# Moving two loads of x to earlier bundles in a hand-scheduled convolution and channel-mix kernel

## The chip, the cores and the metric

The kernel runs on one core of one Trainium2 chip. The metric is device time in microseconds (us); of several runs the median is given. A core has five engines that run side by side, each its own list of instructions in order: TensorE (PE) for matmuls, VectorE (DVE), ScalarE (ACT), GpSimd (POOL), and SyncE (SP), which here only issues transfers. Transfers run on 16 DMA engines that all issuers share.

## The reference

The input x has 8 batches of 4160 tokens with 192 channels. First a causal convolution over 7 tokens, with one softmax-normalized filter for each of 8 heads of 24 channels; then an RWKV channel mix on its result y.

```python
w = softmax(weight)                              # 8 heads x 7 taps
y = causal_conv(x, w)                            # per head, along the tokens
y_prev = y shifted by one token
xk = mu_k * y + (1 - mu_k) * y_prev
xr = mu_r * y + (1 - mu_r) * y_prev
k = relu(xk @ w_k)                               # 192 -> 1024
v = (k * k) @ w_v                                # 1024 -> 192
out = sigmoid(xr @ w_r) * v                      # float32, (8, 4160, 192)
```

## The kernel before

The batches are worked in four pairs. For each pair the tokens go in steps of 512 (`steps`), and a step of two batches is cut into 8 slots, each a matmul of xk with one part of w_k. Four slots make a *bundle*; there are 65 bundles, numbered from 0, and the second half of the second pair's work begins with bundle 24, the third pair's work with bundle 32. The order of the work is written out by hand: tables (`early`, `mix_a`, `late` and others) hold, for each bundle, the functions to call, and `bundle_rest` emits one bundle, in the middle of the kernel always in the same way: on PE two slots of `k_mm` (L593), the first half of an output tile (`v_rows`, L681, tile ps_v), a slot, the gate's matmuls (`r`, L650), a slot, a convolution unit if one is due (`conv_sparse`, L364, tile ps_c), then the second half of `v_rows`. ACT empties the tiles (`k_relu` L605, `r_out` L661, the casts of L337). DVE squares (L619), multiplies the output (`v_out`, L697), and builds xk and xr from y (`diff` L536, `scale` L567, `add_y` L573).

The convolution runs ahead of this. Its input is cut into *groups* of tokens, numbered 0 to 12. Groups 6, 7 and 8 belong to the second pair, 9 and 10 to the third, and from 8 on each group holds 2080 tokens of both batches of the pair. A group goes through five stations, each at a bundle of its own:

- `x_tile` takes a tile for x (tag `xb`, two buffers, so group 9 takes the one that groups 6 and 7 used), writes two elements of it with a DVE memset (L125) and, where the group starts its batch, clears 32 rows on POOL (L127).
- `load_x` issues the loads from POOL, one call for each of the two batches of the pair: for a group at the start of its batch a small first piece (L148) and four large ones (L154) of up to 240 KB as written to the tile. Before the second batch's call, `tie_x` writes two elements of the second batch's part with a DVE memset (L113); the first large load of that batch has to wait for it, so that the loads cannot be issued before DVE has reached that place in its order.
- `conv_sparse` is called four times, for two heads each, at bundles 14 to 17 for group 8 and 22 to 25 for group 9. Each call reads both batches.
- `y_write` writes y to DRAM from SP, 8 transfers, at the end of the last of those bundles (17 for group 8, 25 for group 9).
- `y_read` reads it back with a transposing transfer, also from SP, in two halves: for group 8 at the end of bundles 19 and 22. `diff` reads the result two bundles before the step that needs it; for the first half of group 8 that is in bundle 22.

What stands in the table `early` is called first in its bundle. The DMA transfers of POOL carry eight completion counters in turn, and a transfer waits until the previous one on its counter is complete.

Of the kernel before, what the change touches and what calls it, by code (L numbers as in the profile page):

```python
# [14 lines left out]
def kernel(  # L15
# [719 lines left out]
    def at(table, b, fn, *a):  # L735
        table.setdefault(b, []).append((fn, a))
# [7 lines left out]
    for g, (p, base, nb, fb, on_pe) in enumerate(groups):  # L744
        if g < 3:
            continue
        if p == 0:
            xs = {3: [1, 1], 4: [2, 2, 3, 3], 5: [4, 4, 5, 5]}[g]
        elif g not in sparse:
            xs = [fb - 9] * 2 + [fb - 7] * 2  # L750
        else:
            xs = {8: [14, 15, 16, 17], 9: [22, 23, 24, 25]}.get(g, [fb - 13, fb - 11, fb - 9, fb - 7])
        for i, b in enumerate(xs):
            xt.setdefault(b, []).append((g, i))
        if not on_pe:
            at(late, xs[-1], y_write, g)
        if g in sparse:
            at(late, max(fb - 5, xs[-1] + 2), y_read, g, slice(0, 1), 2)
            at(late, fb - 2, y_read, g, slice(1, 2), 2)
            b, b1 = {8: (9, 12), 9: (18, 21), 10: (24, 25)}.get(g, (fb - 19, fb - 16))  # L760
            at(early, b, x_tile, g)
            at(early, b, load_x, g, (0,))
            b = b1
            at(early, b, tie_x, g, 1)
            at(early, b, load_x, g, (1,))
            continue
        if not on_pe:
            at(mix_c if g == 4 else late, xs[-1] + (1 if g < 6 else 2), y_read, g)
        if g > 4:

            b = {5: 1, 6: 3, 7: 7}.get(g)
            b = first_bundle[first_step[p]] + (-15, -11, -7, -3)[(g - 6) % 4] if b is None else b
            table = {5: mix_a, 7: mix_c}.get(g, early)
            at(table, b, x_tile, g)
            at(table, b, load_x, g)
    for s, (p, t0, L, n0, ns) in enumerate(steps):
        fb = first_bundle[s]
# [27 lines left out]
    for s, j, vb in quads:  # L805
        b = vb - (s == LAST)
        if 0 < s < LAST - 1:
            b = min(b, first_bundle[s + 2] - 2 + j)
# [255 lines left out]
```

## Time and profile before

| | |
|---|---|
| median of 3 runs | 420.95 us (418.74 to 421.1) |
| the profiled execution's own time | 419.52 us |
| its span, first to last instruction | 417.7 us |
| mean granted TensorE clock | 0.992 |
| busy share of PE, DVE, ACT, POOL | 97%, 89%, 85%, 14% |
| PE L681 (ps_v) | 4032 matmuls, 190.0 us |
| PE L593 (ps_k) | 1632 matmuls, 192.5 us |
| PE L364 (ps_c) | 640 matmuls, 10.0 us, 4.2 us idle before them |
| x loads from POOL, 240 KB each | 52, median 8.2 us from issue to landing |

The profile was taken from one execution; all its times are microseconds from the span's start. "Busy" is time in which an engine executes instructions, and matmuls overlap in the pipeline, so that their single times may sum to more than the time that passes. "Idle before" is time in which the engine stood still ahead of an instruction, and the releaser behind the arrow is what ended it. The granted clock is the share of its full clock that TensorE had.

### The profile page before, as it was taken

The page shows a single profiled execution, that of the slowest core. Times are in us where ns is not written, and L with a number is a line of the kernel's source. Part 1 is how long each engine was busy: PE and PEld are TensorE (multiplying, and loading weights), DVE is VectorE, ACT ScalarE, POOL GpSimd, SP SyncE. Part 2 cuts the span into 40 slices and gives each one's busy share as a digit, 9 for nine tenths or more (in the row PEclk, how much of TensorE's full clock was granted, in tenths as well). Part 3 has the DMA queues.
Part 4 walks back from the last instruction along what each step waited for, and adds up shares of the span by engine and source line. Part 5 has one row for each costly group of instructions (what it writes and reads, how often), then busy time and mean ns, then how long its engine had stood idle before and what let it go on. Part 6 is the DMA issues. An engine that isn't in the chain of part 4 may idle for free.

```text
span 417.7 us, 17418 instructions
## 1 busy us (share of the span) xinstructions
PE 404.1 (97%) x7669; PEld 304.2 (73%) x7670; DVE 372.2 (89%) x672; ACT 354.8 (85%) x426; POOL 57.4 (14%) x91
## 2 busy tenths in 40 slices
PE   7899999999999969999999999999999999999996
PEld 5567767777867746777777777777777787777895
DVE  5999799998999966899999999999999999999973
ACT  6899988889998857989898988988989788787781
POOL 8622022030021202203120020300000001000000
PEclk9999999999999988999999999999999999999999
DMA  9999989997729993998997999959432767212223
GB/s 146 193 196 186 194 193 202 233 195 177 158 58 191 232 230 70 190 233 185 194 147 164 196 188 201 168 139 213 119 111 66 204 158 156 78 52 66 77 78 115
DMA packets 139091, 66.35 MB, mean 159 GB/s; under 512 B 89332, under 2 KB 139016, under 8 KB 139016
## 3 DMA queue, kind: packets, MB, share of 16 engines
q1 hardware_dynamic: 95672, 48.32, 47.7%
q0 software_dynamic: 42544, 16.36, 33.8%
q8 instruction: 60, 0.98, 1.0%
q10 hardware_dynamic: 800, 0.57, 0.5%
q14 instruction: 15, 0.12, 0.1%
HBM read 33.29 MB, written 36.99 MB: 168 GB/s over the span
## 4 chain that ended last, share of the span: by engine, by line
PE 62%; DMA 3%; DVE 0%; issue 0%
PE ps_v L681 28%; PE ps_k L593 26%; PE ps_r L650 5%; DMA xb<-in_x_dram 3%; PE ps_c L364 1%; PE ps_v L633 1%; DVE o_sb L717 0%
## 5 line engine op out<-in xcount | busy, mean ns | idle before, releaser
L605 ACT ACTIVATE k_sb<-ps_k 128x1024 bf16<-128x1024 f32 x260 | 253.4, 1039 | 37.5 <-PE ps_k L593 36.8
L619 DVE TENSOR_TENSOR k<-k_sb 128x1024 bf16<-128x1024 bf16 x260 | 173.6, 688 | 25.6 <-ACT k_sb L605 25.5
L593 PE MATMUL ps_k<-xk,wk 64*128 64x512 bf16 (+1 forms) x1632 | 192.5, 368 | 1.6 <-DVE xk L573 1.5
L681 PE MATMUL ps_v<-wv,k 64*128 64x192 bf16 x4032 | 190.0, 244 | 0.2 <-DVE k L619 0.2
L681 PEld LDWEIGHTS <-k 64*128 64x128 bf16 x4032 | 169.6, 94 | 13.4 <-issue 5.0
L593 PEld LDWEIGHTS <-wk 64*128 64x128 bf16 x1632 | 83.9, 94 | 57.5 <-issue 4.2
L697 DVE TENSOR_TENSOR o_sb<-ps_v,r_sb 128x768 f32<-128x768 f32 x64 | 60.9, 951 | 8.9 <-PE ps_v L681 6.5
L154 POOL DMA_DIRECT2D xb<-in_x_dram x62 | 43.9, 718 | 143.6 <-DVE xb L113 59.8
L661 ACT ACTIVATE r_sb<-ps_r 128x768 bf16<-128x768 f32 x65 | 53.5, 825 | 8.8 <-PE ps_v L681 7.2
L337 ACT CAST y<-ps_c 128x960 bf16<-128x960 f32 (+2 forms) x84 | 52.8, 709 | 3.8 <-PE ps_c L364 3.8
L650 PEld LDWEIGHTS <-xr 64*128 64x128 bf16 x780 | 34.9, 94 | 14.9 <-issue 1.3
L650 PE MATMUL ps_r<-wr,xr 64*128 64x192 bf16 x780 | 43.3, 243 | 0.5 <-DVE o_sb L697 0.5
L567 DVE TENSOR_SCALAR xr<-d,mu 128x512 bf16<-128x512 bf16 (+1 forms) x102 | 36.0, 357 | 0.0
L536 DVE TENSOR_TENSOR d<-yT 128x1536 bf16<-128x1536 bf16 (+4 forms) x36 | 31.2, 867 | 2.1 <-ACT yT L423 1.5
L567 DVE TENSOR_SCALAR xk<-d,mu 128x512 bf16<-128x512 bf16 (+1 forms) x99 | 32.7, 360 | 0.1
L573 DVE TENSOR_TENSOR xr<-xr,yT 128x1536 bf16<-128x1536 bf16 (+1 forms) x33 | 31.1, 942 | 1.1
L573 DVE TENSOR_TENSOR xk<-xk,yT 128x1536 bf16<-128x1536 bf16 (+3 forms) x33 | 30.6, 927 | 0.1
L520 POOL COPY y_tail<-yT 128x195 bf16<-128x195 bf16 x4 | 2.9, 721 | 88.6 <-DMA yT<-y_dram 88.6
L364 PE MATMUL ps_c<-xb,toe 32*32 32x240 bf16 x640 | 10.0, 270 | 4.2 <-DMA xb<-in_x_dram 3.8
L364 PEld LDWEIGHTS <-toe 32*32 32x32 bf16 x640 | 4.4, 88 | 13.0 <-issue 11.9
L127 POOL MEMSET xb<- 32x384 bf16 x3 | 1.2, 408 | 63.5 <-DVE xb L125 56.2
L413 PEld LDWEIGHTS <-xb 128*32 128x32 bf16 (+3 forms) x264 | 4.9, 112 | 2.5 <-ACT xb L247 1.3
(58 smaller groups left out, 65.1 us busy)
## 6 DMA issues: line engine op xcount, KB each, us to landing
out_dram<-o_sb SPq DMA_DIRECT2D x128, 192.0 KB
xb<-in_x_dram POOLq DMA_DIRECT2D x52, 240.0 KB, 8.2
y_dram<-y SPq DMA_DIRECT2D x40, 195.0 KB
y_dram<-y SPq DMA_DIRECT2D x16, 210.0 KB
xb<-in_x_dram POOLq DMA_DIRECT2D x4, 228.0 KB, 5.6
xb<-in_x_dram POOLq DMA_DIRECT2D x4, 192.0 KB, 6.1
wk<-in_moe_w_k_dram POOLq DMA_DIRECT2D x4, 192.0 KB, 6.0
xb<-in_x_dram POOLq DMA_DIRECT2D x2, 216.0 KB, 5.1
```

What stands on the lines that cost most here:

```text
L154: nc.gpsimd.dma_start(out=xb[q0 : q0 + rows, lo:hi, s, :], in_=bass.AP(tensor=x.tensor, offset=x.offset + (b * S + t0 + lo * step) * D, ap ...
L337: nc.scalar.copy(out=bass.AP(tensor=y.tensor, offset=y.offset + d, ap=[y.ap[0], [m * 2 * D, 2], [2 * D, m], [Q, 2], [1, b - a]],), in_=bas ...
L536: nc.vector.tensor_tensor(out=shaped(s, diffs[s][:, cs, :L]), in0=y_of(s, cs, 1), in1=y_of(s, cs, 0), op=ALU.subtract)
L567: nc.vector.tensor_scalar(out=t[:, c, :L], in0=diffs[s][:, c, :L], scalar1=mu[:, i, c : c + 1], scalar2=None, op0=ALU.mult)
L573: nc.vector.tensor_tensor(out=o, in0=o, in1=y_of(s, sl, 0), op=ALU.add)
L593: nc.tensor.matmul(out=ps[:, i, f * L : (f + 1) * L], lhsT=wk[r, c, fs], rhs=xk[r, c, :L], start=c == 0 and f == 0, stop=c == NC - 1 and f ...
L605: nc.scalar.activation(out=k_sb, in_=ps.rearrange("p a b -> p (a b)"), func=AF.Relu)
L619: nc.vector.tensor_tensor(out=o, in0=i, in1=i, op=ALU.mult)
L650: nc.tensor.matmul(out=ps[:, i, k * D : (k + 1) * D], lhsT=xr[q, c, ts], rhs=wr[q, c, :], start=c == 0, stop=c == NC - 1,)
L661: nc.scalar.activation(out=r_sbs[s, j], in_=r_ps.pop((s, j))[:, :, 0 : 2 * D], func=AF.Sigmoid)
L681: nc.tensor.matmul(out=v_ps[s, j][:, bank, k * D : (k + 1) * D], lhsT=k2s[s][q, f, t * P : (t + 1) * P], rhs=wv[q, f, :], start=half == 0 ...
L697: nc.vector.tensor_tensor(out=o_sb.rearrange("p (b t) d -> p b (t d)", b=2), in0=v_ps.pop((s, j)), in1=r_sbs.pop((s, j)), op=ALU.mult,)
```

## The change

For group 9 the pair of bundles at which the loads of its two batches are called becomes (17, 18) instead of (18, 21). `x_tile` and the first batch's `load_x` move from bundle 18 to 17; `tie_x` and the second batch's `load_x` move from bundle 21 to 18. All stay first in their bundles. No other group's entry is touched.

```diff
         if g in sparse:
             at(late, max(fb - 5, xs[-1] + 2), y_read, g, slice(0, 1), 2)
             at(late, fb - 2, y_read, g, slice(1, 2), 2)
-            b, b1 = {8: (9, 12), 9: (18, 21), 10: (24, 25)}.get(g, (fb - 19, fb - 16))
+            b, b1 = {8: (9, 12), 9: (17, 18), 10: (24, 25)}.get(g, (fb - 19, fb - 16))
             at(early, b, x_tile, g)
             at(early, b, load_x, g, (0,))
             b = b1
             at(early, b, tie_x, g, 1)
             at(early, b, load_x, g, (1,))
             continue
```

## The prediction

> **What bounds the kernel now.** I read first the page's busy line and its forty slices. PE is busy for 97% of the span, so time can only come out of a place where PE waits or runs slowly; the other engines have 11% or more to spare.
>
> ```profile
> PE 404.1 (97%) x7669; PEld 304.2 (73%) x7670; DVE 372.2 (89%) x672; ACT 354.8 (85%) x426; POOL 57.4 (14%) x91
> PE   7899999999999969999999999999999999999996
> PEclk9999999999999988999999999999999999999999
> ```
>
> Between the two ends there is one dent: the fifteenth slice (146.2 to 156.6 us) holds a PE digit of 6, and in it and the next the granted clock falls to 8. Who is waited for there, the list of waits says (engine, line, releaser: total us, times, longest). Cut to 160 us and later, the same list has no PE wait at all.
>
> ```profile
> PE ps_c L364 <- DMA xb<-in_x_dram: 3.8, 2, 2.6
> ACT y L337 <- PE ps_c L364: 3.8, 1, 3.8
> ```
>
> Then PE's order of time. A bundle runs from one first-half ps_v burst to the next, so bundle 22 runs from 148.48 to 161.24; its convolution (L364) is the first unit of group 9, the third pair's first group.
>
> ```profile
> 148.48 1.50 PE L681 MATMUL ps_v<-wv,k 64*128 64x192 bf16 x32
> ...
> 150.55 0.29 PE L364 MATMUL ps_c<-xb,toe 32*32 32x240 bf16 x8
> 152.06 0.28 PE L364 MATMUL ps_c<-xb,toe 32*32 32x240 bf16 x4 [1.21 <-DMA xb<-in_x_dram]
> 154.95 0.59 PE L364 MATMUL ps_c<-xb,toe 32*32 32x240 bf16 x20 [2.61 <-DMA xb<-in_x_dram]
> 155.47 2.74 PE L681 MATMUL ps_v<-wv,k 64*128 64x192 bf16 x32
> ...
> 161.24 1.48 PE L681 MATMUL ps_v<-wv,k 64*128 64x192 bf16 x32
> 163.30 0.42 PE L364 MATMUL ps_c<-xb,toe 32*32 32x240 bf16 x32
> 163.66 1.49 PE L681 MATMUL ps_v<-wv,k 64*128 64x192 bf16 x32
> ```
>
> The same work in bundle 23 has no gap in its convolution. Which load was late, GpSimd's order of time says: the last four x loads before the stall are issued at 140.52, released by the memset of L113, which ties them to DVE's place in bundle 21.
>
> ```profile
> 122.73 0.41 POOL L127 MEMSET xb<- 32x384 bf16 x1 [34.61 <-DVE xb L125]
> 123.43 0.54 POOL L148 DMA_DIRECT2D xb<-in_x_dram  x1 [0.29 <-POOL xb L127]
> 123.96 2.75 POOL L154 DMA_DIRECT2D xb<-in_x_dram  x4
> 126.70 0.53 POOL L148 DMA_DIRECT2D xb<-in_x_dram  x1
> 140.52 2.75 POOL L154 DMA_DIRECT2D xb<-in_x_dram  x4 [13.29 <-DVE xb L113]
> ```
>
> They land up to 154.9 (the chain that ended last has this load as a piece of 12.32 us from 142.58). On SP the first transposing read of group 8 is issued at 136.93 for 5.93 us; from 142 to 144 the DMA view shows 2266 packets of SP's queue and none of GpSimd's, so the x loads stand behind it. The second such read is issued at 148.91.
>
> **The price of the stall.** By stages (us, then the five engines, PEclk, DMA share, GB/s):
>
> ```profile
> 148.48:161.24 12.76, 8.94 (x137) 6.00 (x134) 6.39 (x11) 6.53 (x8) 0.00 (x0) 0.73 0.98 192
> 161.24:167.47 6.23, 6.23 (x138) 4.46 (x134) 5.43 (x11) 5.90 (x10) 2.69 (x4) 1.00 0.33 40
> 167.47:173.89 6.42, 6.42 (x137) 4.57 (x134) 5.80 (x12) 6.42 (x10) 2.71 (x4) 1.00 1.33 182
> ```
>
> These bundles do the same PE work (137 or 138 matmuls in the records). Bundle 22 takes 12.76 - 6.23 = 6.53 us more than 23. By parts: the two waits are 1.21 + 2.61 = 3.82; from the second ps_v burst to the bundle's end it takes 161.24 - 155.47 = 5.77 against 167.47 - 163.66 = 3.81, so 1.96 for the slow clock; the convolution's own matmuls at that clock take the other 0.74. Bounds from neighbours: against bundle 24 the excess is 6.34; against bundle 16 (113.24 to 119.17, 5.93) it is 6.83.
>
> The clock part stands on a row: in the stage from 155.00 to 159.30 the granted clock is 0.50, after two idle pieces of 1.21 and 2.61 us. The Trainium skill ("TensorE: Matmul & The Clock Gate", section "HAM oscillation — how this bites in real kernels") asks for no idle gap above some 3.4 us; read strictly, gaps of 1.21 and 2.61 would leave the clock alone and only 3.82 us would come back. The trace disagrees, since the clock did fall, and I go by the trace.
>
> **The change part by part.** Nothing is added or removed; the order of the built kernels is the same on POOL, SP and ACT, and on DVE two memsets of 59 ns move.
>
> *First batch, 18 to 17.* The memset of L125 moves from 122.53 to its place between the last two squarings of the bundle before, about 116.1 (DVE starts a squaring at 115.41 and the next at 116.48, after 0.39 idle). The memset on POOL (0.41), one issue of L148 (0.54), four of L154 (2.75) and the second batch's first piece (0.53) follow, so issues run from about 116.9 to 120.7 instead of 123.43 to 127.2. POOL has idled since 88, so nothing is queued behind them. The buffer was last read by group 7's convolution, whose last matmul is at 95.7: no new wait on DVE or POOL. From 115 to 119 no DMA packet moves, so these 0.97 MB find empty engines; before, they went out beside group 8's write-back (SP, 123.24 for 8.77 us).
>
> *Second batch, 21 to 18.* The memset of L113 takes the old place of L125, 122.53, so the four L154 issue from 122.6 to 125.4, some 18 us earlier. The last of them waits on the counter of the first batch's first large load; with that issued near 117.4 and the landings of this batch before at 9.4 to 11.7 us, it would be held to at most 129.1. The slowest x load of the trace landed after 14.1 us: 143.2 at worst, against a need at 150.55. The wait is therefore gone, with 7 us to spare; the conv of bundles 23 to 25 reads the same tile and needs nothing more.
>
> *What the loads now stand beside.* Group 8's write-back at 123.24 has the second batch beside it in place of the first: the same four or five transfers, 0.96 against 0.97 MB. What can be added is what remains of the first batch by then: nothing, or at most all of it, 0.97 MB at the 200 GB/s of the stage 124 to 139, 4.9 us. I take 1 us, since it has six us of free engines. The write-back feeds the first transposing read, whose packets end near 144, and DVE wants it at 150.31 (L536): slack 6.2 us, so either bound is covered. Were that cover gone, each us late would stop DVE and then PE for one us. From 140 to 155 the output writes and both transposing reads lose a megabyte of competition; this is off PE's path and I count it as nothing.
>
> *What is late next.* Group 10's loads hang on DVE in bundles 24 and 25 and move 6.5 us forward with everything else, to about 158; the second transposing read, issued at 148.91, was through at 157.4 in spite of the x loads. Its reader is four bundles later. All later stages keep their mutual distances.
>
> **The sum.** Against the profiled execution (span 417.7, its own time 419.52): 3.82 + 1.96 + 0.74 = 6.52 less, hence 413.0 and a span near 411.2. Its time is 1.43 under the median of the runs shown (420.95); from the median it is 414.4. I take the middle, 413.7. The likeliest case alone spans 411.9 (fastest run 418.74 less 6.83) to 414.6 (median less 6.34).
>
> **The rivals.**
> 1. *The gain is only part.* The transposing read of group 8 slips past 150.31 and DVE waits at L536 in bundle 22. Against it: 6.2 us of slack against at most 4.9 of extra bytes; for it: the write-back's issues on SP took 0.33 to 2.1 us each, so SP's queue does stretch. At 8 to 10 us of slip, 2 to 4 us are lost and 413.7 becomes 416 to 418.
> 2. *Nothing to be had.* The unprofiled runs do not have this stall, because their loads land in time: 420 to 421. For it: landings hang on what else is in flight. Against: the profiled run is inside the range of the others, not above it.
> 3. *Slower.* The same place as in 1, but so crowded that the read is more than 6.2 + 6.5 = 12.7 us late: then a DVE stall and a cold PE cost more than the old wait. At 16 us it is 413.7 + 9.8, near 423.5, plus a clock loss like the 2.7 now: 426. It would need some three times the bytes that the change moves.
> 4. *The load moves but lands late again.* It would have to take 25 us from issue, against 14.1 at most; no chance worth naming.
>
> **How the numbers follow.** Likeliest case 0.78, rival 1 0.08, rival 2 0.08, rival 3 0.06. The range goes from 411.5, a little under the case's 411.9 since three runs do not bound the spread, up to 417.1, the median less the 3.82 of the waits alone (all clock loss back elsewhere), which takes in half of rival 1. One per cent, about what a measurement of this kernel tells from no change, is 4.2 us. Faster by more: 0.78 + 0.05 of rival 1 = 0.83; within: 0.03 + 0.08 + 0.02 of rival 3 = 0.13; slower: 0.04.
>
> **What would show it.** In the profile of the changed kernel: first x loads issued near 117 and the tied four near 122.6; no PE wait on x in the list; PE digits of 9 throughout the middle; granted clock 1.00 from 150 to 160; bundle 22 in 5.9 to 6.4 us; span near 411.2. I am wrong if DVE waits for the transposing read at L536, if the x wait turns up again at L364, or if the dent goes and the timed runs still stand near 420.

## The result, and the profile after

The changed kernel takes 414.66 us as the median of 4 runs (412.98 to 414.86), the kernel before, in 4 runs beside it, 420.65: a ratio of 0.9857, 95% interval 0.9817 to 0.9898. So it is 1.4% faster. In this document a median takes in every run of a kernel, while a ratio leaves out the few runs that lie more than 1.5% above the fastest of their kernel. Its profiled execution took 412.98 us with a span of 411.3, against 419.52 and 417.7 before.

The page's busy line and slices of the changed kernel:

```profile
PE 401.3 (98%) x7670; PEld 302.5 (74%) x7670; DVE 371.1 (90%) x672; ACT 354.6 (86%) x426; POOL 57.8 (14%) x91
PE   7899999999999999999999999999999999999996
PEclk9999999999999999999999999999999999999999
```

The 6 in the fifteenth slice is gone, and so are the two 8s of the clock. The same stretch in PE's order of time, and the stages of bundles 22 and 23 (us, busy time of PE, PEld, DVE, ACT, POOL, then PEclk, DMA share, GB/s):

```profile
148.52 1.50 PE L681 MATMUL ps_v<-wv,k 64*128 64x192 bf16 x32
150.59 0.42 PE L364 MATMUL ps_c<-xb,toe 32*32 32x240 bf16 x32
150.95 1.50 PE L681 MATMUL ps_v<-wv,k 64*128 64x192 bf16 x32
...
154.72 1.48 PE L681 MATMUL ps_v<-wv,k 64*128 64x192 bf16 x32
```

```profile
148.52:154.72 6.20, 6.20 (x138) 4.53 (x134) 5.97 (x11) 5.99 (x8) 0.00 (x0) 1.00 0.72 173
154.72:161.05 6.33, 6.33 (x136) 4.59 (x134) 5.87 (x11) 6.33 (x10) 2.60 (x4) 1.00 0.54 111
```

Bundle 22 starts at 148.52, as before (148.48), runs its convolution in one piece of 0.42 us, and is over after 6.20 us instead of 12.76: 6.56 less, which is the whole gain of the span (6.4). From the end of bundle 25 to the end of the span it takes 411.3 - 173.70 = 237.6 us now, and took 417.7 - 180.13 = 237.6 before. The loads and the read, in the order of time of POOL and of SP:

```profile
116.41 0.41 POOL L127 MEMSET xb<- 32x384 bf16 x1 [28.12 <-DVE xb L125]
117.11 0.60 POOL L148 DMA_DIRECT2D xb<-in_x_dram  x1 [0.29 <-POOL xb L127]
117.70 2.77 POOL L154 DMA_DIRECT2D xb<-in_x_dram  x4
120.46 0.53 POOL L148 DMA_DIRECT2D xb<-in_x_dram  x1
123.09 2.89 POOL L154 DMA_DIRECT2D xb<-in_x_dram  x4 [2.10 <-DVE xb L113]
```

```profile
123.42 7.05 SPq L466 DMA_DIRECT2D y_dram<-y  x8
130.56 4.83 SPq L705 DMA_DIRECT2D out_dram<-o_sb  x4
135.48 7.52 SPq L488 DMA_TRANSPOSE yT<-y_dram  x1
```

The second batch's four large loads are issued 17.4 us earlier, and by the trace's packets the last x packet moves at 139.8 instead of 154.5. The first transposing read of group 8 (called *the read* from here on) has its last packet at 145.8, 1.4 us later than before (144.4), and DVE wants it at 150.35.

### The profile page after: what moved, and what is told of

Read it like the earlier page. It is cut to its first block, busy times and chain, and to the rows that moved or that the text cites. A ratio compares the mean times of both kernels' runs of the same rounds, so it can differ in the third digit from the quotient of the medians.

```text
span 411.3 us, 17419 instructions
## 1 busy us (share of the span) xinstructions
PE 401.3 (98%) x7670; PEld 302.5 (74%) x7670; DVE 371.1 (90%) x672; ACT 354.6 (86%) x426; POOL 57.8 (14%) x91
## 4 chain that ended last, share of the span: by engine, by line
PE 87%; DMA 4%; DVE 4%; ACT 2%; POOL 1%; issue 1%; SPq 0%; POOLq 0%; ACTq 0%
PE ps_v L681 39%; PE ps_k L593 37%; PE ps_r L650 7%; PE ps_c L364 2%; DMA yT<-y_dram 2%; DMA wk<-in_moe_w_k_dram 2%; DVE k L619 2%; PE ps_v L633 1%; ACT k_sb L605 1%; DMA y_dram<-y 1%; PE ps_c L319 1%; ACT y L337 0%; DVE d L536 0%; POOL xb L154 0%; SPq L479 0%
```

## The experiments

The table sums up what the profiles show of this one meeting place. "Loads" is when the second batch's large loads start to be issued, "read on SP" how long the read occupies SP's list; packets are those of the trace (256 bytes for the read, 384 for x), their times to within 0.1 us. The waits are those of bundles 20 to 22, in the one profiled execution of each kernel.

| kernel, bundles of group 9 | loads | read on SP | read's packets | last x packet | waits, us |
|---|---|---|---|---|---|
| before (18, 21) | 140.52 | 5.93 | 139.0-144.4 | 154.5 | PE for x 3.8 |
| after (17, 18) | 123.09 | 7.52 | 137.5-145.8 | 139.8 | none |
| first only (17, 21) | 141.14 | 3.82 | 136.5-140.5 | 151.2 | none |
| second only (18, 18) | 126.55 | 12.96 | 138.2-151.4 | 150.0 | DVE for output buffer 2.0, for the read 0.2; PE behind DVE 2.0 |
| (18, 20) | 135.11 | 14.46 | 142.4-154.7 | 153.7 | DVE for output buffer 1.9, for the read 3.8; PE for x 0.6, behind DVE 4.1 |
| (17, 20) | 135.81 | 5.84 | 137.1-148.3 | 154.0 | PE for x 2.3 |
| (16, 17) | 116.77 | 4.50 | 136.6-140.4 | 128.9 | none |
| (17, 18), read at 20 | 122.60 | 5.96 | 140.1-146.1 | 140.8 | DVE for output buffer 0.8; PE behind DVE 0.8 |
| (17, 18), read at 21 | 123.96 | 3.35 | 145.9-149.4 | 140.9 | DVE for output buffer 0.2 |
| (18, 21), read at 21 | 140.30 | 9.12 | 148.6-153.9 | 151.6 | PE for x 1.2, DVE for the read 5.5; PE behind DVE 3.5 |

**The first batch's move alone.**

```diff
-            b, b1 = {8: (9, 12), 9: (18, 21), 10: (24, 25)}.get(g, (fb - 19, fb - 16))
+            b, b1 = {8: (9, 12), 9: (17, 21), 10: (24, 25)}.get(g, (fb - 19, fb - 16))
```

> Bundles (17, 21): only the first batch's load is moved. Theory (the whole gain is the lateness of the second batch's four loads, which the moved call of bundle 21 still issues near 140.5, behind the first transposing read of group 8): the PE wait at L364 of bundle 22 stays at 3 to 4 us, the granted clock still falls to 0.5 after it, span 417 to 418.5, time within 1% of the kernel before. Rival (the crowd: the gain comes from taking the first batch out of the write-back's way, so that everything behind it on the DMA engines is earlier): the wait shrinks below 1.5 us and the span falls by 3 us or more.

Measured: 415.64 us median, ratio 0.9883 (0.9855 to 0.991), span 412.9, granted clock 1.00. My theory fell here and the rival held: the second batch's loads are issued at the old place and PE does not wait.

```profile
141.14 2.75 POOL L154 DMA_DIRECT2D xb<-in_x_dram  x4 [19.67 <-DVE xb L113]
```

```profile
135.08 3.82 SPq L488 DMA_TRANSPOSE yT<-y_dram  x1
```

By these lines of POOL and SP the read has left SP before the loads are issued. In the kernel before, the first batch had gone out beside group 8's write-back until 139.8, the read had come out at 139.0 to 144.4, and the loads that were issued at 140.52 had moved no packet before 144.2. With the first batch through by 128.6, the read's packets end at 140.5 and the loads run from 142.6 to 151.2, which is just enough: the convolution takes 0.79 instead of 0.42 us.

**The second batch's move alone.** Same line, `9: (18, 18)`.

> Bundles (18, 18): only the second batch's load is moved, so that all 1.9 MB go out beside the write-back of group 8. Theory: the full gain, no PE wait at L364, span 410.8 to 412, ratio 0.983 to 0.988; the transposing read may end 1 to 3 us later than near 144 but still ahead of 150.3. Rival (the first batch's move is needed, since two batches beside the write-back make the transposing read late): DVE waits at L536 in bundle 22 for 1 to 4 us, span 412.5 to 416.

Measured: 416.22, ratio 0.9899 (0.9867 to 0.9931), span 415.2. Neither case as written: PE has no wait for x, and DVE waits for the read only 0.2 us, but a new wait stands elsewhere. From the waits between 136 and 180 us, then SP's order of time and DVE's line of the wait:

```profile
DVE o_sb L697 <- DMA out_dram<-o_sb: 2.0, 1, 2.0
PE ps_r L650 <- DVE o_sb L697: 2.0, 1, 2.0
```

```profile
132.19 3.65 SPq L705 DMA_DIRECT2D out_dram<-o_sb  x4
135.88 12.96 SPq L488 DMA_TRANSPOSE yT<-y_dram  x1
148.93 4.35 SPq L705 DMA_DIRECT2D out_dram<-o_sb  x6
```

```profile
142.55 0.96 DVE L697 TENSOR_TENSOR o_sb<-ps_v,r_sb 128x768 f32<-128x768 f32 x1 [2.05 <-DMA out_dram<-o_sb]
```

The read stays on SP for 12.96 us, and x packets move until 150.0. `v_out` has to wait for one of its three output buffers, which holds up PE by 2.0 us. The wait ends at 142.55, while SP is still in the read, so the output writes that DVE waited for had left SP ahead of the read, by 135.84. They were late on the DMA engines, where x packets moved beside them; that the x packets made them late was not tried by itself. Between 165 and 177 us PE has two more pieces of idle time, 1.2 and 0.8 us; neither ends on a DMA, and their cause stays open, so not all of the 3.9 us by which this span is longer than the changed kernel's is explained.

**The second batch one bundle earlier than before.** Same line, `9: (18, 20)`.

> Bundles (18, 20): the second batch goes out one bundle earlier than in the kernel before, near 134.4 instead of 140.5, ahead of the first transposing read's packets (138 to 144) instead of behind them. Theory (the loads stand behind the read): most packets move before 142, the last lands by about 147, no PE wait at L364, span 410.8 to 412.5. Rival (a plain matter of 6.1 us: the loads take the same 14.4 us from issue to the last landing): landing near 148.8, also no wait. Second rival (the read, put behind more load packets, is late): DVE waits at L536 in bundle 22, up to 2 us. The landing time tells the first two apart: under 12.5 us from the first issue to the last landing for the theory, 14 or more for the rival.

Measured: 417.27, the median of ten runs that spread from 414.48 to 421.24, ratio 0.99 (0.9867 to 0.9932). The profiled execution, 421.24, is the longest of the ten, so its waits need not be those of the usual run. In it the second rival came true, and in a size that I had not given it (3.8 us against at most 2). DVE's order of time:

```profile
143.83 0.96 DVE L697 TENSOR_TENSOR o_sb<-ps_v,r_sb 128x768 f32<-128x768 f32 x1 [1.86 <-DMA out_dram<-o_sb]
...
156.78 0.96 DVE L536 TENSOR_TENSOR d<-yT 128x1536 bf16<-128x1536 bf16 x1 [3.78 <-DMA yT<-y_dram]
```

Loads and read start together, and both come late: 18.6 us from the first issue of the loads to the last x packet, longer than either the theory or the first rival had it, and 14.46 us of the read on SP.

**The second read out of the way.**

```diff
-            at(late, fb - 2, y_read, g, slice(1, 2), 2)
+            at(late, fb - 2 + (g == 8), y_read, g, slice(1, 2), 2)
```

> The kernel before with bundles (18, 21), but the second transposing read of group 8 at the end of bundle 23 instead of 22; its reader is the diff of bundle 26. Theory (the last x packets of 152 to 154.9 are held by this second read, which starts near 152): without it the loads are through by 152 to 153, the PE wait at L364 falls from 3.8 to 1 to 2.5 us, and the span to 414 to 416. Rival (the first read alone makes them late, the second does nothing): wait 3.5 to 4, span 417 to 418.5.

Measured: 419.37, ratio 0.9983 (0.9951 to 1.0014), span 418.0, PE's wait for x 3.2 instead of 3.8, last x packet at 153.9 instead of 154.5. The rival held in the main: between these two profiles the wait differs by 0.6 us, so the second read is not what makes the loads late.

**The idle time filled.** Ahead of the convolution of bundle 22 of the kernel before:

```diff
+        if b == 22:
+            warm(ring.tile([P, 2, BANK], FP32, tag="k", name="fill"), 18)
         for u in units:
             if u[0] in sparse:
```

> The kernel before with bundles (18, 21), and 18 matmuls of zeros (128 columns by 512) ahead of the convolution of bundle 22, into a tile that nothing reads; at some 0.216 us each they fill 3.9 us, the length of the two waits. The loads of x land as before, so the convolution still ends near 155.5. Theory (2.7 of the 6.5 us are the slow clock that the idle time brings): the granted clock stays at 1.00 through 150 to 160, bundle 22 takes some 10.0 to 10.5 us instead of 12.76, span 414.5 to 415.8, ratio 0.991 to 0.995. Rival (the slow clock is not due to the waits, or costs nothing since other engines are behind anyway): the clock falls all the same or the bundle stays near 12.5, span 417 to 418.5.

Measured: 417.5, ratio 0.9955 (0.9917 to 0.9993), span 415.7. Stage of bundle 22, in the columns as above:

```profile
149.07:159.26 10.19, 10.14 (x154) 6.12 (x152) 6.26 (x11) 6.40 (x8) 0.00 (x0) 1.00 1.13 211
```

```profile
155.14 0.42 PE L364 MATMUL ps_c<-xb,toe 32*32 32x240 bf16 x32
155.50 1.49 PE L681 MATMUL ps_v<-wv,k 64*128 64x192 bf16 x32
...
159.26 1.48 PE L681 MATMUL ps_v<-wv,k 64*128 64x192 bf16 x32
```

The clock stays at 1.00 and the bundle takes 12.76 - 10.19 = 2.57 us less, with matmuls that do nothing in the place of the wait. Of this, 2.01 us lie behind the convolution: from the second ps_v burst to the bundle's end it takes 159.26 - 155.50 = 3.76 us instead of 5.77. The other 0.56 us lie ahead of it and are not all the clock, since this bundle also began 0.59 us later (149.07 against 148.48) while the last x packet moved only 0.2 us later. So the slow clock is worth between 2.0 and 2.6 us of the stall, and the rest is the wait itself.

**The read one bundle later in the changed kernel.**

```diff
-            at(late, max(fb - 5, xs[-1] + 2), y_read, g, slice(0, 1), 2)
+            at(late, max(fb - 5, xs[-1] + 2) + (g == 8), y_read, g, slice(0, 1), 2)
```

> The changed kernel, bundles (17, 18), but the first transposing read of group 8 at the end of bundle 20 instead of 19, some 5.8 us later. It tests the slack of the read that the prediction's rivals rest on. Theory (slack 6.2 us, in the changed kernel about 6 as the read ends near 144.3): the read ends near 150, DVE waits at L536 in bundle 22 for 0 to 1 us, span 411 to 412.5, no difference from the changed kernel above 0.3%. Rival (the slack is smaller than read from the packets, because landing is only known to DVE some us after the last packet): a DVE wait of 1.5 to 4 us and span 413 to 416.

Measured: 413.79, ratio 0.9841 (0.9785 to 0.9897), span 412.5. The move was worth less than I had put down: the read is issued at 138.51 instead of 135.48, its packets end at 146.1, and DVE does not wait for it in bundle 22. Two bundles earlier DVE waits 0.8 us for an output buffer, and PE behind it. The theory's result holds; the slack was not tried to its end.

**The read two bundles later.** As above, `+ 2 * (g == 8)`.

> The changed kernel, bundles (17, 18), with the first transposing read of group 8 at the end of bundle 21 instead of 19, some 11.5 us later: it makes on purpose the lateness of the slower rival. Theory (past the slack each us late stops DVE and then PE for one us): the read ends near 155.5 to 157, DVE waits 5 to 7 us at L536 in bundle 22, span longer than the changed kernel's by that and up to 2.7 us of slow clock, 416 to 421. Rival (the squarings and multiplications already done carry PE over it): PE loses less than 2.5 us, span under 414.

Measured: 415.34, ratio 0.9884 (0.9833 to 0.9935), span 412.9. There was no lateness to price: the read is issued at 144.50, and with no x load in flight it takes 3.35 us on SP; its packets end at 149.4, ahead of DVE. The rival's number came out, but not for its reason. A bundle of order is not a bundle of time on SP, whose list runs behind.

**The changed kernel and (17, 21) again, on one chip.** The four kernels that follow are compared with the same runs of the kernel before. First the changed kernel once more, unaltered:

> The changed kernel, bundles (17, 18), on one chip with the other edits. Theory as it now stands (the first transposing read of group 8 and x loads that are in flight with it hold each other up; the changed kernel has all of its x loads out of the way early, and its read takes some 7.5 us on SP): ratio 0.984 to 0.987, and at least as fast as (17, 21). Rival (only the first batch's move pays): no difference from (17, 21) above 0.2%.

Then (17, 21) again:

> Bundles (17, 21) on the same chip. Theory: the read is done before the second batch's loads, as in the first look at this kernel, where it took 3.82 us on SP and the loads landed just as the convolution began; with no slack left in that, some runs wait 0 to 2 us: ratio 0.986 to 0.990, slower than (17, 18) by 0.5 to 2 us. Rival (only the first batch's move pays): the same as (17, 18) within 0.2%.

Measured: 415.38, ratio 0.9866 (0.9834 to 0.9899) for the changed kernel, and 413.82, ratio 0.9843 (0.9813 to 0.9873) for (17, 21). The intervals overlap for most of their length, and the medians stand the other way round than my theory had them. Once the first batch has moved, the second batch's move brings nothing that these runs can tell.

**The second batch between the two.** Same line, `9: (17, 20)`.

> Bundles (17, 20): the second batch one bundle earlier than in (17, 21), two later than in (17, 18). Its four loads are issued near 135, together with the first transposing read. Theory (read and loads hold each other up when they are in flight together): the read takes 8 to 14 us on SP instead of 3.8, its packets end at 147 to 153, DVE waits for it or for the buffers of the output writes queued behind it, and the span is 1 to 5 us longer than with either (17, 18) or (17, 21): 413 to 417. Rival (earlier is better, the read does not mind): the read stays under 6 us on SP and the span is at or under 412.9.

Measured: 416.46, ten runs from 412.23 to 420.32, ratio 0.9861 (0.9826 to 0.9895); the profiled execution has a span of 416.6. Between two places that both work, 18 and 21, lies one that is worse in its profile and unsteady, though its ratio is not told apart from theirs. The profile shows the third longest of the ten, 418.29. The read takes only 5.84 us on SP, against my 8 to 14, but its packets are spread over 11.2 us, and the loads are last at 154.0, so that in this execution the loads lose:

```profile
151.86 0.31 PE L364 MATMUL ps_c<-xb,toe 32*32 32x240 bf16 x12
154.45 0.39 PE L364 MATMUL ps_c<-xb,toe 32*32 32x240 bf16 x20 [2.28 <-DMA xb<-in_x_dram]
```

**Both batches earlier still.** Same line, `9: (16, 17)`.

> Bundles (16, 17): both batches one more bundle earlier, so that they are through by about 127, nearly all before the write-back of group 8. Theory (with the PE wait gone nothing is left to win here): PE as in the changed kernel, span 411 to 412.5, the read 3.5 to 6 us on SP, time within 0.2% of (17, 18). Rival (the remaining traffic beside the write-back still costs): 1 us or more faster than (17, 18).

Measured: 414.42, ratio 0.985 (0.9818 to 0.9882), span 412.6, no PE wait in bundle 22, read of 4.50 us on SP. With the loads through by 128.9 the read is nearly as quick as in (17, 21) (3.82), and the time is that of the changed kernel. These runs show nothing left to win at this place.

**The read moved away from the loads in the kernel before.** The edit of the read by two bundles, with (18, 21).

> The kernel before, bundles (18, 21), x loads as they were, but the first transposing read of group 8 at the end of bundle 21 instead of 19, so that the second batch's loads, issued at 140.5, no longer stand behind it. Theory (the read of 139 to 144.4 is what kept these loads from starting before 144.2): their packets start by 142.5 and most are through before the read's; the PE wait at L364 falls from 3.8 to 0 to 2 us; but the read now has loads beside it and may end past 150.3, with a DVE wait at L536 of 0 to 4 us. Span 412 to 417. Rival (the loads are slow for the bytes of all queues, wherever the read stands): the last load lands at 154 or later and PE waits 3 us or more.

Measured: 421.22, ratio 1.0 (0.9965 to 1.0036), span 420.2. Waits between 140 and 165 us:

```profile
DVE d L536 <- DMA yT<-y_dram: 5.5, 1, 5.5
...
PE ps_r L650 <- DVE o_sb L697: 3.7, 2, 3.5
...
PE ps_c L364 <- DMA xb<-in_x_dram: 1.2, 1, 1.2
```

With no read in front of them, the same loads issued at the same time move from 141.7 to 151.6, and PE's wait for them falls from 3.8 to 1.2. Now the read is late in its turn: DVE waits 5.5 us for it, PE 3.5 us in one piece, and the stage that follows runs slow:

```profile
155.88 0.96 DVE L536 TENSOR_TENSOR d<-yT 128x1536 bf16<-128x1536 bf16 x1 [5.53 <-DMA yT<-y_dram]
```

```profile
159.23 0.78 PE L650 MATMUL ps_r<-wr,xr 64*128 64x192 bf16 x12 [3.48 <-DVE o_sb L697]
159.77 2.80 PE L681 MATMUL ps_v<-wv,k 64*128 64x192 bf16 x32
...
163.81 1.49 PE L681 MATMUL ps_v<-wv,k 64*128 64x192 bf16 x32
```

```profile
148.43:159.77 11.34, 6.68 (x138) 4.59 (x135) 5.81 (x11) 7.78 (x9) 0.00 (x0) 0.99 1.15 207
159.77:163.45 3.68, 3.68 (x42) 2.92 (x37) 2.86 (x6) 0.81 (x1) 0.24 (x1) 0.55 0.33 107
```

This is the shape of the prediction's slower rival, and here it eats the whole gain: from the start of bundle 22 to that of bundle 24 it takes 167.61 - 148.43 = 19.18 us, against 18.99 in the kernel before.

## Why the prediction was right, and where not

*The bound and the stall.* Right. The only dent in PE's work was the whole of what the change could give, and it gave it: 6.56 us in bundle 22 against 6.53 in the sum, and nothing elsewhere.

*The clock term.* Right in kind, and about right in size: 1.96 us behind the convolution in the sum, 2.01 in the filled kernel. The 0.74 us of the convolution's own matmuls are only in part the clock: in (17, 20), at a clock of 1.00, a convolution broken by one wait takes 0.31 + 0.39 = 0.70 us instead of 0.42. The sum does not suffer, since its parts add up to the measured excess of the bundle. The sum by the waits alone, 3.82 us, would have been 2.7 us short.

*Which edit pays.* Here the working failed. The sum puts the whole gain on the second batch's earlier issue ("The wait is therefore gone"), and treats the first batch's move as a swap beside the write-back ("the same four or five transfers", "I take 1 us"). The runs show that each edit removes the wait for x by itself, by different ways: the second because its loads are through before they are needed, the first because the write-back and then the read get out of the way of loads that are still issued at the old time (in (17, 21) the read's packets end at 140.5 instead of 144.4). The cause of the wait was not the time of issue alone but that x loads and the read met: in the kernel before, no x packet moved from 139.8 until 144.2, with loads issued at 140.52, while in (17, 21) the first packet moved 1.4 us after the issue. Moving the read alone took away 2.6 of the 3.8 us. The prediction saw that the loads stood "behind it" and did not follow what set the read's time. The sum came out all the same, since both edits were made and either brings the one gain that there is.

*What the loads stand beside.* I allowed the read 1 us more and at most 4.9; it ended 1.4 us later. As the second batch alone shows, the range for that was too narrow in general: with both batches beside the write-back the read ended at 151.4, 7 us later than before, beyond the 6.2 us of slack. Bytes divided by a mean rate do not bound what a transposing read loses to loads in flight. The slack itself was counted from the read's last packet, and DVE began its `diff` 2.0 us after that packet in (18, 20) and in the last experiment, 0.5 in (18, 18), so it was up to 2 us smaller. The loss of (18, 18), 2.0 us of PE, came from a place that no rival had: the output buffers.

*The slower rival.* Its place was real, and so was its price: in the last experiment 5.5 us of DVE's wait made bundle 22 longer by 11.34 - 6.23 = 5.1 us. PE's wait for x, 1.2 us, lies inside DVE's and adds nothing, as PE had to wait for DVE afterwards. The slow stretch behind it, from bundle 23's first to its second ps_v burst, took 163.81 - 159.77 = 4.04 instead of 2.42 us, 1.6 more. That is nearly one for one, with the clock on top, as the rival had it. The changed kernel stayed clear of it by 150.35 - 145.8 = 4.5 us, counted from the last packet.

*The number.* The profiled execution came out at 412.98 against 413.0 worked out for it. The median lies 1.68 us above it, as it lay 1.43 above before, so the sum made from the median (414.4) was the better one; the middle, 413.7, halved a gap that did not go away. Why the other runs take longer than the profiled one stays open. The lower bound 411.9 leans on bundle 16, which is no like neighbour: its stage has 127 matmuls, not 137 or 138.

## What to carry to other kernels

When a load is late, look at what it meets on the way before pricing its issue: here a transfer of another queue, kept late by an earlier load, did most of the damage, and moving either load cured it. A step moved "a little earlier" may land on exactly what it ought to avoid; try the places on both sides, as a curve with a dip in it cannot be seen from its two ends. And price a PE stall with the slow clock behind it, which was worth 2.0 to 2.6 of 6.5 us here.

## What was not expected of the hardware

A transposing read and x loads in flight together slow each other beyond what their bytes ask for. While the read's packets moved, all queues together moved 173, 141 and 126 GB/s in (18, 18), (18, 20) and (17, 20), where 0.54 to 0.67 MB of x went out beside it, and 220 to 245 GB/s in (17, 21) and (16, 17), where none did. The time that the read occupies SP shows this only in part: 3.3 to 4.5 us in (17, 21), (16, 17) and the changed kernel with the read at 21, with no x load beside it, and 13.0 and 14.5 in (18, 18) and (18, 20), but only 5.84 in (17, 20), although four large loads were in flight there too. So which of the two loses differs between (18, 20) and (17, 20), and the times are unsteady: 412.2 to 420.3 us for (17, 20), where (17, 18), (17, 21) and (16, 17) spread over 1.4 to 3.4. That the same thing changes sides from run to run is likely but not shown, as each kernel has one profile.

The clock after short idle pieces does not follow one length. After 2.28 us of waiting for x, (17, 20) kept a clock of 1.00, while (18, 20) fell after 2.28 us of waiting for DVE, to a mean of 0.58 in the stage behind it:

```profile
149.78:158.53 8.75, 6.47 (x137) 4.54 (x134) 6.26 (x11) 6.40 (x8) 0.00 (x0) 1.00 1.26 252
```

```profile
160.62:164.10 3.48, 3.48 (x43) 2.41 (x38) 2.92 (x6) 0.81 (x1) 0.00 (x0) 0.58 0.80 211
```

The traces also record when the granted clock changes. In the middle of the kernels each slow stretch lasts 3.41 us or twice that, and all changes of a trace lie a multiple of 3.41 us apart. With such a grid the two cases differ: the idle piece of (18, 20) lies whole in one stretch of the grid, at whose end, 161.2, the clock fell, while that of (17, 20) is cut into 1.27 and 1.00 us. In the kernel before the clock fell at 152.8, inside the second wait, after a stretch with 1.58 us idle; with the read moved away it fell at 159.7, after one with 2.99; the 2.00 us of (18, 18), of which 1.33 lay in one stretch, left it alone. That the idle time within one stretch decides fits these cases, but no run was made to test it, and there is no fixed bound: near its end the kernel before has a stretch with 1.88 us idle and no fall behind it. The Trainium skill ("TensorE: Matmul & The Clock Gate", section "What's actually happening") describes a free-running window of about 3.4 us; the runs agree with the window's length, and not with reading it as the least idle time that matters.
